# An mLSTM cell in front of a leaky-relu FFN on one core: transfers moved to ScalarE's queue, broadcasts joined into one request, and the last group's first product in float32r

## The chip, the cores and the metric

The kernel runs on one core of one Trainium2 chip. Times are device microseconds of one execution. The core's engines are TensorE (PE; its weight loads are listed apart as PEld), VectorE (DVE), ScalarE (ACT), GpSimd (POOL) and SyncE (SP). Each takes its instructions in order. Transfers are asked for by an engine's queue (SP's and ScalarE's here; a request is an instruction on that engine) and are carried out by sixteen DMA engines that the queues share.

## The reference

```
for t in range(768):                       # per batch b (4) and head h (8), head size D = 40
    m_new  = maximum(f[t] + m, i[t])
    f_stab = exp(f[t] + m - m_new);  i_stab = exp(i[t] - m_new)
    C = f_stab * C + i_stab * outer(v[t], k[t])
    n = f_stab * n + i_stab * k[t]
    y[t] = sigmoid(o[t]) * (C @ q[t]) / maximum(abs(n . q[t]), 1)
x = y as 3072 tokens x 320 features
h = x @ w_in                               # 320 x 2048
g = maximum(0.01 * h, h)
return g @ w_out                           # 2048 x 320
```

All inputs and the output are f32.

## The kernel before, in words

**Chunks, steps, groups.** The 768 tokens of a batch are cut into `NB` = 6 chunks `c` of 128. A step `s = 4*c + b` is one chunk of one of the four batches. The cell is computed chunk by chunk in matrix form with a state carried between chunks; the FFN of chunk `g` (its four steps together, 512 tokens, a "group") runs while the cells of chunk `g + 1` are computed. A loop (lines 1043 to 1103) gives out the work: 30 units of FFN for each group, 16 for the first product and 14 for the second, and after chosen units (`pairs`, line 1041) a piece of the next chunk's cells. The last group has no cells beside it.

**Order.** TensorE, DVE, ScalarE and POOL run in the order in which the program issues (`manual_schedule`, line 1022). SP's requests are ordered by the scheduler. A DMA signals on one of eight semaphore lanes, given out in turn, so that a request also waits until the DMA eight before it has landed.

**FFN.** The first product (`ff_units`, line 753) has eight pairs `j`: two PSUM banks `ph`, five slots of 64 rows on each of two row groups, 512 tokens moving (line 759), and a relu of each bank on ScalarE into `acts` (line 767). The second product (`fast_units`, line 824) is a fast scheme of seven products instead of eight, each for two token blocks `n`: p1, p1, p2, p2, p6, p6, p7, p7, p4, p4, p5, p5, p3, p3, eight matmuls each (line 835). Each product fills a bank `po`, which is emptied by ScalarE (p1, p6, p7, p4: copies at 854, 867, 875, 881) or DVE (p2, p5, p3: additions at 862, 887, 892). `ph` and `po` share the four banks of the pool `psf` in turn. The cells use four other banks, pool `psc`.

**Cells.** `load` (344) brings k with one request (356) and the values with four (359). `spread` (406) and `spread_q` (415) broadcast a row of gate factors of each batch from the scratch `a_dr` in HBM to 64 partitions, twice, into `w` and `ea` (lines 413 and 421). `u_mix` (684) multiplies state and gate-weighted queries (695), normalizes on DVE and POOL (702 to 713) and stores the step's x in the scratch `x_dr` with four requests of 20 rows (716). `gather_x` (719) reads it back with four requests (730) into `xT`, where the FFN of the next group reads it; it runs after the last unit of the first product (index 15) and later. All these requests are on SP. The last two steps' mixes stand after unit 19.

**Which lines the text uses.** 759 and 767 (first product, relu), 835 (second), 854 to 892 (its sums), 695 to 730 (mix, store, gather), 356, 359, 413, 421 (loads and broadcasts), 450 (POOL's product with `w`), 822 to 870 (DVE's sums of `acts` and weights), 249 to 263 (the weights' splitting at the start: masks, scaled sums, differences on DVE), 641 (a product with 128-column weights and 41 moving columns).

Of the kernel before, what the change touches and what calls it, by code (L numbers as in the profile page):

```python
# [10 lines left out]
U32 = mybir.dt.uint32  # L11
U64 = mybir.dt.uint64
AF = mybir.ActivationFunctionType
ALU = mybir.AluOpType
# [4 lines left out]
def kernel(  # L19
# [58 lines left out]
    dr = ctx.enter_context(tc.tile_pool(name="dr", bufs=1, space=bass.MemoryType.DRAM))  # L78

# [39 lines left out]
    kn = consts.tile([P, NL, H, DP], F32, name="kn")  # L119
    qn = consts.tile([P, NL, H, DP], F32, name="qn")  # L120
    S_t = [consts.tile([P, 2, H, DP], F32, name=f"S{n}") for n in range(NL)]
    S_v = [t[:].rearrange("p u h (k d) -> p u h k d", d=QW) for t in S_t]
    rb_t = [consts.tile([P, 3, RW], F32, name=f"rb{n}") for n in range(NR)]
    xb = consts.tile([P, PR * TB, QW], F32, name="xb")
# [147 lines left out]
    def gates(c):  # L272


        m0 = m0s.get(c)
        n = P if c == 0 else BH
        fc, il = (f0[:], i0[:]) if c == 0 else (fi[c][:, 0, :], fi[c][:, 1, :])
        F = wk.tile([n, P], F32, name="F", bufs=1)
        nc.vector.tensor_tensor_scan(F[:], fc, zeros[:n].to_broadcast([n, P]), 0.0, op0=ALU.add, op1=ALU.add)
        if c > 0:  # L280
            il_t = wk.tile([BH, P], F32, name="il", bufs=1)
            nc.vector.tensor_scalar(il_t[:], il, scalar1=m0[:], scalar2=None, op0=ALU.subtract)
            il = il_t[:]
        m = wk.tile([n, P], F32, name="m", bufs=1)
        nc.vector.tensor_tensor_scan(m[:], fc, il, -1e30 if c == 0 else 0.0, op0=ALU.add, op1=ALU.max)
        a = wk.tile([n, P], F32, name="a", bufs=1)
        nc.vector.tensor_tensor(a[:], F[:], m[:], op=ALU.subtract)
        bu = wk.tile([BH, 3, P], F32, name="bu", bufs=1)
        nc.vector.tensor_tensor(bu[:, 0, :], il[:BH], F[:BH], op=ALU.subtract)
        if c + 1 < NB:  # L290
            m1 = wk.tile([BH, 1], F32, name="m0")
            if c == 0:
                nc.vector.tensor_copy(m1[:], m[:BH, P - 1 :])
            else:
                nc.vector.tensor_tensor(m1[:], m0[:], m[:, P - 1 :], op=ALU.add)
            m0s[c + 1] = m1
        if c > 0:
            na = wk.tile([BH, 1], F32, name="na")
            nc.vector.tensor_tensor(na[:], m[:, SL - 1 : SL], F[:, SL - 1 : SL], op=ALU.subtract)
        bus[c] = bu, a, (na if c > 0 else None)  # L300

    def gates_exp(c):
# [9 lines left out]
        if c > 0:  # L312
            nc.sync.dma_start(a_dr[c, 0].rearrange("u n t -> n u t"), a[:].rearrange("n (u t) -> n u t", u=2))
            if c > 1:
                nc.sync.dma_start(a_dr[c, 1].rearrange("u n t -> n u t"), bu[:, 2, :].rearrange("n (u t) -> n u t", u=2))
            if 1 < c < NB - 2:
                load_fi(c + 2)
# [25 lines left out]

    def load(s):
        c, b = divmod(s, B)
        rows = ts(c, P)
        d = st.setdefault(s, {})
        n = s % NL
        d.update(k=kn[:, n], q=qn[:, n])
        if c == 0:  # L350
            d["va"] = S_t[n][:, 1]
            parts = [(d["k"][:, :, :D], k), (d["q"][:, :, :D], q), (d["va"][:, :, :D], v)]
            for dst, src in parts:
                nc.sync.dma_start(dst, src[b, :, rows, :].rearrange("h p d -> p h d"))
            return
        nc.sync.dma_start(d["k"][:, :, :D], k[b, :, rows, :].rearrange("h p d -> p h d"))
        for u in range(2):
            for i in range(2):
                nc.sync.dma_start(  # L359
                    S_v[n][ts(u, SL), u, :, i, :DB],  # L360
                    v[b, :, c * P + u * SL : c * P + (u + 1) * SL, DB * i : DB * (i + 1)].rearrange("h p d -> p h d"),
                )
# [42 lines left out]

    def spread(s):
# [3 lines left out]
        w = wk.tile([P, H, P], F32, name="w", bufs=NL)  # L410
        d["w"] = w[:].rearrange("p h t -> p (h t)")[:, : H * SL].rearrange("p (h t) -> p h t", t=SL)
        for u in range(2):
            nc.sync.dma_start(d["w"][ts(u, SL)], a_dr[c, 0, u, b * H : (b + 1) * H, :].partition_broadcast(SL))

    def spread_q(s):
# [3 lines left out]
        d["ea"] = wk.tile([P, H, SL], F32, name="ea", bufs=EAB)  # L419
        for r in range(2):  # L420
            nc.sync.dma_start(
                d["ea"][ts(r, SL)], a_dr[c, 1, 1 - r, b * H : (b + 1) * H, :].partition_broadcast(SL),
            )

    def spread_first(a, s2):
# [12 lines left out]
        for n in range(2):  # L438
            w = st[s2 + n]["w"] = wk.tile([P, H, P], F32, name="w", bufs=NL)
# [20 lines left out]
    def prep_vu(s):  # L460
# [3 lines left out]
        if s < NS:  # L464
            d["vu"] = wk.tile([P, H, 2, V1], F32, name="vu")
# [34 lines left out]
    def prep_kq(s):  # L500

        d = st[s]
        d["kqT"] = wk.tile([P, 2, PR * P], F32, name="kqT")
# [20 lines left out]
    def u_split(s):  # L524

        d = st[s]
        d["kqT"] = wk.tile([P, 2, PR * P], F32, name="kqT")
# [14 lines left out]
    def u_transpose(s):  # L542
        d = st[s]
        d["kqT"] = wk.tile([P, 2, PR * P], F32, name="kqT")
# [92 lines left out]
    def u_values(s):  # L637
# [4 lines left out]
        d["den"] = wk.tile([P, H], F32, name="den")  # L642
        denominators(d["den"][:], pa[:, :, D])

    def gate(s):

        d = st[s]
        d["x"] = wk.tile([P, Dm], F32, name="x")
# [7 lines left out]
    def u_plain(s):  # L656
# [13 lines left out]
        den = wk.tile([P, H], F32, name="den")  # L670
        denominators(den[:], hN[:, :, 0, DB])
        if b < 2:
            d["x"] = wk.tile([P, Dm], F32, name="x")[:]
# [10 lines left out]
    def u_mix(s):  # L684
# [16 lines left out]
        hb = wk.tile([P, PR * TB, QW], F32, name="hb", bufs=1)  # L701
        nc.vector.transpose(hb[:].rearrange("p (j n) d -> p j n d", n=TB), in_blocks(pT[:]))  # L702
        den = wk.tile([P, PR * TB], F32, name="den")
# [8 lines left out]
        xq = wk.tile([P, PR * P], F32, name="x")  # L712
# [6 lines left out]
    def gather_x(s):  # L719

        c, b = divmod(s, B)
        if ("xT", c) not in st:
            st["xT", c] = wk.tile([P, KC, GT], F32, name="xT", bufs=1)
        xT = st["xT", c]
        src = x_dr[s].rearrange("(k p) t -> p k t", p=DP)
        for r in range(2):
            at = 0
            while at < KC:
                k0, n = run_of(r, at)
                nc.sync.dma_start(xT[DP * r : DP * (r + 1), at : at + n, ts(b, P)], src[:, k0 : k0 + 2 * n - 1 : 2, :])  # L730
                at += n

# [20 lines left out]
    def ff_units(g):  # L753
        xT = st["xT", g]
# [59 lines left out]
        return firsts + fast_units(g)  # L814
# [104 lines left out]
    def ahead(s):  # L919

        if s < NS:
            if s < 2 * B:
# [99 lines left out]
    with tc.manual_schedule(engines={E.PE, E.DVE, E.Activation, E.Pool}):  # L1022
# [20 lines left out]
        for c in range(1, NB + 1):  # L1043
            if c > 1:
                ffs = ff_units(c - 1)
            cells = cell_units(c) if c < NB else []
            n_ff, n_c = len(ffs), len(cells)
            done = fed = 0
            waiting, after = [], []
            for i in range(n_ff):  # L1050
                if c == 1:
                    run(now, 2 if i < 10 else 3 if i < 14 else 4)
                    for n in fetch.get(i, ()):
                        load_weights(QN + n)
                    if i == 0:
                        prep_mask(B)
                        ahead(B)
                        load_fi(3)
                for s, steps in lazy.items():
                    if s in late and late[s] > 0:  # L1060
                        late[s] -= 1
                    else:
                        run(steps, 3)
                for n in masks.get(i, ()) if 1 < c < NB else ():
                    if c * B + n < NS:
                        prep_mask(c * B + n)
                ffs[i]()
                if c + 1 < NB:
                    if i == (1 if c == 1 else 0):
                        gates(c + 1)  # L1070
                    if c == 2 and i == 0:
                        mixed_weights()
                    if i == (3 if c == 1 else 2):
                        gates_exp(c + 1)
                upto = min(n_c, sum(p <= i for p in (place if c == 1 else pairs)))
                while done < upto:
                    fn, s = cells[done]
                    fn(s)
                    done += 1
                    if fn is u_mix:  # L1080
                        waiting.append(s)
                    if fn is u_plain and s < 2 * B - 1 or fn is u_parts and s == 2 * B - 1:
                        ahead(s + 1)
                    elif fn is u_mix:
                        after.append(s + 2)
                    elif fn is u_plain:
                        prep_mask(s + 2)
                        ahead(s + 2)
                if i >= NF - 1:
                    for s in waiting:  # L1090
                        gather_x(s)
                    waiting.clear()
                if i < NF or i >= NF + 8:
                    for s in after:
                        ahead(s)
                    after.clear()
                while fed < done:
                    fn, s = cells[fed]
                    fed += 1
                    if fn in (u_mix, u_plain):  # L1100
                        load_late(s + NR, 2)
                        if s + NL < NS:
                            feed(s + NL)
# [31 lines left out]
```

## Time and profile before

| what | us | where it is from |
|---|---|---|
| median of 3 runs | 511.85 | times (510.85 to 513.27) |
| the profiled execution's span | 508.0 | the page |
| TensorE busy | 492.0 (97%) | the page |
| DVE, ScalarE, POOL busy | 308.1, 171.5, 137.7 | the page |
| groups 1 to 4 of the FFN, start | 139.3, 214.2, 289.0, 365.2 | the trace's timeline |
| last group: start, first product, second product | 439.8, 34.5, 30.6 | the chain |

The runs' median is 3.85 us above the span of the one profiled execution; the span counts from the first to the last instruction that the trace records. A row of a group of instructions gives line, engine, operation, tiles and shape, count, then busy time and mean length, then the engine's idle time just before with what released it. The chain is read from top to bottom in time: start, length, what ran.

### The profile page before, as it was taken

The page shows a single profiled execution, that of the slowest core. Times are in us where ns is not written, and L with a number is a line of the kernel's source. Part 1 is how long each engine was busy: PE and PEld are TensorE (multiplying, and loading weights), DVE is VectorE, ACT ScalarE, POOL GpSimd, SP SyncE. Part 2 cuts the span into 40 slices and gives each one's busy share as a digit, 9 for nine tenths or more (in the row PEclk, how much of TensorE's full clock was granted, in tenths as well). Part 3 has the DMA queues.
Part 4 walks back from the last instruction along what each step waited for, and adds up shares of the span by engine and source line. Part 5 has one row for each costly group of instructions (what it writes and reads, how often), then busy time and mean ns, then how long its engine had stood idle before and what let it go on. Part 6 is the DMA issues. An engine that isn't in the chain of part 4 may idle for free.

```text
span 508.0 us, 12526 instructions
## 1 busy us (share of the span) xinstructions
PE 492.0 (97%) x4981; PEld 366.6 (72%) x4981; DVE 308.1 (61%) x515; ACT 171.5 (34%) x478; POOL 137.7 (27%) x175
## 2 busy tenths in 40 slices
PE   8878999999999999999999999999899999999997
PEld 7766878767655489955589855599755599744797
DVE  4779898899954778635765826764825664101321
ACT  3664864652722510323411323311213411022210
POOL 4243443360402404413104614014612003000020
PEclk9877999999999999999999999999999999999999
DMA  9977687888765551565663566564466212200001
GB/s 116 146 204 154 149 219 185 168 152 175 155 145 87 131 124 46 133 130 144 147 132 92 115 137 170 137 141 97 109 135 177 68 53 62 69 1 1 1 1 52
DMA packets 165290, 59.21 MB, mean 117 GB/s; under 512 B 128816, under 2 KB 156016, under 8 KB 165232
## 3 DMA queue, kind: packets, MB, share of 16 engines
q1 hardware_dynamic: 164848, 58.28, 52.2%
q8 instruction: 39, 0.64, 0.5%
q14 instruction: 19, 0.16, 0.1%
q10 hardware_dynamic: 384, 0.13, 0.1%
HBM read 51.68 MB, written 6.70 MB: 115 GB/s over the span
## 4 chain that ended last, share of the span: by engine, by line
PE 79%; DVE 9%; DMA 3%; ACT 3%; POOL 2%; issue 2%; SPq 2%; ACTq 0%; POOLq 0%; DVEq 0%
PE ph L759 36%; PE po L835 26%; PE po L794 6%; PE pT L695 3%; PE sd L614 3%; SPq L359 1%; PE sd L619 1%; DMA S<-in_v_dram 1%; ACT kqT L540 1%; PE tkq L548 1%; DVE raw L261 1%; DMA rb<-in_q_dram 1%; DMA w<-a_dr 1%; PE pa L641 1%; DVE qn L511 1%
## 5 line engine op out<-in xcount | busy, mean ns | idle before, releaser
L759 PE MATMUL ph<-xT,w_in 64*128 64x512 f32 (+1 forms) x1120 | 216.2, 538 | 2.4 <-DVE y L887 1.4
L759 PEld LDWEIGHTS ph<-xT,w_in 64*128 64x128 f32 x1120 | 108.6, 189 | 95.1 <-issue 86.3
L767 ACT ACTIVATE acts<-ph 128x512 f32<-128x512 f32 (+1 forms) x112 | 53.9, 533 | 179.0 <-PE ph L759 178.9
L835 PEld LDWEIGHTS po<-w_out,acts 128*128 128x128 f32 x640 | 87.3, 190 | 3.8 <-issue 3.8
L835 PE MATMUL po<-w_out,acts 128*128 128x160 f32 x640 | 89.1, 300 | 0.0
L450 POOL TENSOR_TENSOR w<-w,i 128x512 f32<-128x512 f32 x20 | 26.9, 1345 | 117.3 <-DMA w<-a_dr 117.2
L624 DVE TENSOR_TENSOR qn<-w,sd 64x512 f32<-64x512 f32 x40 | 27.4, 684 | 40.2 <-PE sd L619 20.5
L458 ACT ACTIVATE w<-w,gT 128x64 f32<-128x64 f32 (+1 forms) x192 | 50.8, 348 | 2.7 <-POOL w L450 1.7
L592 POOL TENSOR_TENSOR S<-S,f 40x336 f32<-40x336 f32 x36 | 32.0, 889 | 67.3 <-PE pT L695 36.3
L835 PE MATMUL po<-raw,acts 128*128 128x160 f32 x320 | 45.5, 300 | 0.0
L835 PEld LDWEIGHTS po<-raw,acts 128*128 128x128 f32 x320 | 43.9, 190 | 0.3
L794 PE MATMUL po<-w_out,acts 128*128 128x320 f32 x128 | 36.5, 436 | 0.0
L702 DVE STREAM_TRANSPOSE hb<-pT 128x512 f32<-128x512 f32 x16 | 11.5, 717 | 31.0 <-PE pT L695 30.8
L794 PEld LDWEIGHTS po<-w_out,acts 128*128 128x128 f32 x128 | 23.6, 190 | 9.3 <-issue 0.3
L511 DVE TENSOR_TENSOR qn<-kqT,ea 64x512 f32<-64x512 f32 x32 | 28.4, 888 | 1.0
L709 POOL TENSOR_TENSOR xb<-xb,den 128x320 f32<-128x320 f32 x16 | 11.7, 729 | 56.8 <-DVE xb L706 56.6
L596 DVE TENSOR_TENSOR S<-S,sd 40x336 f32<-40x336 f32 x36 | 18.1, 503 | 12.1 <-POOL S L592 11.2
L614 PEld LDWEIGHTS sd<-kqT 40*64 40x64 f32 x640 | 19.9, 135 | 6.1 <-issue 6.1
L822 DVE TENSOR_TENSOR raw<-acts 128x1024 f32<-128x1024 f32 x10 | 11.8, 1222 | 18.3 <-ACT acts L767 18.2
L713 DVE STREAM_TRANSPOSE x<-xb 128x512 f32<-128x512 f32 x16 | 18.2, 1140 | 7.6 <-POOL xb L709 7.6
L835 PE MATMUL po<-raw 128*128 128x160 f32 x160 | 22.5, 299 | 0.0
L835 PEld LDWEIGHTS po<-raw 128*128 128x128 f32 x160 | 22.0, 190 | 0.0
(151 smaller groups left out, 551.8 us busy)
## 6 DMA issues: line engine op xcount, KB each, us to landing
w<-a_dr SPq DMA_DIRECT2D x40, 128.0 KB
rb<-in_k_dram SPq DMA_DIRECT2D x64, 80.0 KB
rb<-in_q_dram SPq DMA_DIRECT2D x64, 80.0 KB
rb<-in_o_gate_dram SPq DMA_DIRECT2D x64, 80.0 KB
ea<-a_dr SPq DMA_DIRECT2D x32, 128.0 KB
kn<-in_k_dram SPq DMA_DIRECT2D x24, 160.0 KB
raw<-in_moe_w_out_dram SPq DMA_DIRECT2D x6, 640.0 KB
S<-in_v_dram SPq DMA_DIRECT2D x80, 40.0 KB
```

Source lines behind the costliest of these rows:

```text
L450: nc.gpsimd.tensor_tensor(w, w, cm2.unsqueeze(1).to_broadcast([P, H, SL]), op=ALU.add)
L458: yield nc.scalar.activation(w[:, h, :], w[:, h, :], AF.Exp, bias=gT[c][:, 0, bh : bh + 1], scale=1.0)
L511: nc.vector.tensor_tensor(mixed(s)[rows, 1 - r], d["kqT"][rows, 1].rearrange("p (h t) -> p h t", t=SL), d["ea"][rows], op=ALU.mult,)
L592: nc.gpsimd.tensor_tensor(new, old, g, op=ALU.mult)
L596: nc.vector.tensor_tensor(new, new, st[s]["dC", u], op=ALU.add)
L614: nc.tensor.matmul(bank[1 - u][toks, h, :], lhsT=kqT[rows, 0, ts(h, SL)], rhs=kqT[rows, 1, ts(h, SL)], start=True, stop=True,)
L624: nc.vector.tensor_tensor(mixed(s)[toks, u], w[toks], bank[1 - u][toks], op=ALU.mult)
L713: nc.vector.transpose(in_blocks(xq[:]), xb[:].rearrange("p (j n) d -> p j n d", n=TB))
L759: nc.tensor.matmul(ph[r][:, cols], lhsT=w_row(r, slot, j), rhs=xT[DP * r : DP * (r + 1), slot, cols], start=(slot == 0), stop=(slot == KC ...
L767: nc.scalar.activation(acts[:, f, cols], ph[r][:, cols], AF.Prelu, alpha=0.01)
L794: nc.tensor.matmul(po[n][:], lhsT=acts[:, f, ts(n, P)], rhs=w_out[:, f, :], start=(f == 0), stop=(f == NF - 1),)
L835: nc.tensor.matmul(bank[:], lhsT=left[:, f, :], rhs=right[:, f, :], start=f == 0, stop=f == KH - 1)
```

## The change

1. **Requests on ScalarE.** For chunks 3 and later, k and the values are no longer requested by `load` on SP but held as a generator in `later` and requested on ScalarE's queue: one request after each unit of a first product, two after each unit of a second. `ahead` requests at once what is still held. `gather_x` requests on ScalarE; one mixed step is gathered per unit, from the last unit of the first product.
2. **One request per broadcast.** `spread_rows` writes 128 partitions from two rows with one request where there were two of 64 partitions. The two halves of the second gate factor are stored in swapped order, by two requests instead of one.
3. **The last group's first product.** After two pairs as before, each of the other six pairs is three float32r products: `raw` times `raw` and `low` times `low` in the banks `ph`, `dif` times `dif` in two banks `pe` of `psc`. The mask 0xFFFFF000 keeps the top bits of a number; `low` is what it cuts off (scaled by 4096 for w_in, with its sign turned), and `dif` is the number plus a multiple of that part. A ScalarE copy scaled by -EPS, a DVE scaled sum and a ScalarE relu combine them, each per bank.
4. **Preparing that.** When group 4's mixes are issued (after unit 19), the cells' pools are closed and their memory is given to the parts (`open_parts`). Four requests on SP copy w_in to `raw` (128 x 1280 f32 each). Eight halves of w_in are split, each by a DVE mask, a POOL subtraction, a DVE scaled sum and a ScalarE scaled copy; x is split by three DVE passes for each of four steps. These steps are given out two per unit of group 4's second product and three per unit of group 5's first, behind the products' own work.
5. The unit loop is rewritten (placements as before: 30 per group), and the cells' tiles move to pools of their own, `cc` and `cw`.

```diff
+    def bring_later(n):
+        while n > 0 and later:
+            s = next(iter(later))
+            next(later[s][0], None)
...
+        if c < 3:
+            for _ in bring(nc.sync):
+                pass
+        else:
+            later[s] = [bring(nc.scalar), 5]
...
+    def spread_rows(to, rows):
+
+        nc.sync.dma_start(
+            to.rearrange("p h t -> p (h t)"),
+            rows.unsqueeze(1).to_broadcast([2, SL, H, SL]).rearrange("u p h t -> u p (h t)"),
+        )
...
-        for u in range(2):
-            nc.sync.dma_start(d["w"][ts(u, SL)], a_dr[c, 0, u, b * H : (b + 1) * H, :].partition_broadcast(SL))
+        spread_rows(d["w"], a_dr[c, 0, :, b * H : (b + 1) * H, :])
...
-        for r in range(2):
-            nc.sync.dma_start(
-                d["ea"][ts(r, SL)], a_dr[c, 1, 1 - r, b * H : (b + 1) * H, :].partition_broadcast(SL),
-            )
+        spread_rows(d["ea"][:], a_dr[c, 1, :, b * H : (b + 1) * H, :])
...
-                nc.sync.dma_start(xT[DP * r : DP * (r + 1), at : at + n, ts(b, P)], src[:, k0 : k0 + 2 * n - 1 : 2, :])
+                nc.scalar.dma_start(xT[DP * r : DP * (r + 1), at : at + n, ts(b, P)], src[:, k0 : k0 + 2 * n - 1 : 2, :])
...
+    def top_bits(dst, src):
+        nc.vector.tensor_scalar(
+            dst.bitcast(U32), src.bitcast(U32), scalar1=0xFFFFF000, scalar2=None, op0=ALU.bitwise_and,
+        )
...
+        def first():
+            t = tmp_part()[:].rearrange("p k t -> p (k t)")
+            held.append(t)
+            top_bits(t, src)
+            nc.gpsimd.tensor_tensor(t, t, src, op=ALU.subtract)
+
+        def second():
+            t = held[0]
+            nc.vector.scalar_tensor_tensor(
+                parts["w", "dif"][n][:, at], in0=t, scalar=1.0 + 1.0 / EPS, in1=src, op0=ALU.mult, op1=ALU.add,
+            )
+            nc.scalar.activation(parts["w", "low"][n][:, at], t, AF.Copy, scale=1.0 / EPS)
...
+        top_bits(t, src)
+        nc.vector.tensor_tensor(low, t, src, op=ALU.subtract)
+        nc.vector.scalar_tensor_tensor(
+            parts["x", "dif"][:, :, cols], in0=low.bitcast(F32), scalar=1.0 + 1.0 / EPS, in1=src, op0=ALU.mult, op1=ALU.add,
+        )
...
+            def first():
+                ph.extend(psf.tile([P, GT], F32, name=f"ph{r}", tag="mm") for r in range(2))
+                rows(j, ph, "raw", True, False)
+
+            def second():
+                rows(j, ph, "low", False, True)
+
+            def third():
+                pe.extend(psc.tile([P, GT], F32, name=f"pe{r}", tag="c") for r in range(2))
+                rows(j, pe, "dif", True, True)
+                fs = [acts[:, f_of(r, j), :] for r in range(2)]
+                for r in range(2):
+                    nc.scalar.activation(fs[r], pe[r][:], AF.Copy, scale=-EPS)
+                for r in range(2):
+                    nc.vector.scalar_tensor_tensor(
+                        fs[r], in0=ph[r][:], scalar=1.0 + EPS, in1=fs[r], op0=ALU.mult, op1=ALU.add,
+                    )
+                for r in range(2):
+                    nc.scalar.activation(fs[r], fs[r], AF.Prelu, alpha=0.01)
...
+                gather()
+                if t <= ENDS < upto:
+                    open_parts()
+                    for n in range(QN):
+                        fetch_w_part(n)
+                    todo = split_steps()
+                t = max(t, upto)
+                bring_later(1 if i < len(firsts) else 2)
+                prepare(3 if i < len(firsts) else 2)
```

## The prediction

> **What bounds the kernel now.** First the page's shares, the slices and the chain.
>
> ```profile
> PE 492.0 (97%) x4981; PEld 366.6 (72%) x4981; DVE 308.1 (61%) x515; ACT 171.5 (34%) x478; POOL 137.7 (27%) x175
> PE   8878999999999999999999999999899999999997
> DVE  4779898899954778635765826764825664101321
> PEclk9877999999999999999999999999999999999999
> DMA  9977687888765551565663566564466212200001
> PE 79%; DVE 9%; DMA 3%; ACT 3%; POOL 2%; issue 2%; SPq 2%; ACTq 0%; POOLq 0%; DVEq 0%
> ```
>
> TensorE is the bound: 97% busy, at full clock after the fourth slice. Any gain has to shorten its work; anything that makes it wait is a loss. DVE is light only in the last six slices, the DMA engines only in the last nine. The windows, one per FFN group (busy by engine, clock, DMA share):
>
> ```profile
> 139.30:214.20 74.90, 74.90 (x777) 54.24 (x776) 49.35 (x76) 21.45 (x65) 21.27 (x25) 1.00 0.49 109
> 289.00:365.20 76.20, 74.86 (x775) 54.15 (x774) 46.42 (x78) 21.14 (x64) 23.56 (x26) 1.00 0.58 130
> 365.20:439.80 74.60, 74.54 (x706) 54.11 (x706) 36.74 (x64) 16.26 (x44) 12.17 (x16) 1.00 0.41 100
> ```
>
> TensorE fills each group; the waits that a faster queue could remove are at most 1.3 us in one group. The rest of the view of waits agrees: the largest of TensorE's waits is 1.8 us, and almost all lie in the start-up. SP's waits (second fence) cost nothing: SP does only transfers.
>
> ```profile
> PE ph L759 <- DVE y L887: 1.4, 1, 1.4
> SPq L716 <- DVE x L713: 29.8, 11, 8.6
> SPq L730 <- PE ph L759: 8.6, 1, 8.6
> ```
>
> The first line matters: a group's first product waits for the DVE addition that empties a bank of `psf`. These four banks are handed round in order, so a second product (2.19 us: 30.64/14 below) needs the bank of the product four before it. The end of the chain, and ScalarE in the second half of the fourth group:
>
> ```profile
> 417.86 21.93 PE po L835 x160
> 439.79 34.53 PE ph L759 x160
> 474.33 30.64 PE po L835 x224
> ```
> ```profile
> 420.27 0.30 ACT L867 COPY y<-po 128x160 f32<-128x160 f32 x1 [7.71 <-PE po L835]
> 422.44 0.29 ACT L867 COPY y<-po 128x160 f32<-128x160 f32 x1 [1.88 <-PE po L835]
> 424.62 0.29 ACT L875 COPY hn<-po 128x160 f32<-128x160 f32 x1 [1.88 <-PE po L835]
> ```
>
> Each copy begins the moment its product ends, because ScalarE has nothing else there. SP issues the transfers of x:
>
> ```profile
> 420.85 5.10 SPq L716 DMA_DIRECT2D x_dr<-x  x8
> 426.11 6.08 SPq L730 DMA_DIRECT2D xT<-x_dr  x8
> ```
>
> **Part 1: float32r products, gain.** The last group's first product is 34.53 us for eight pairs, 4.32 each: five slots of two row groups, 0.86 us a slot. Six pairs become three products of five slots. No float32r product is in the trace. The edit splits each operand into a top and a low half; an f32 product is four half-products, so one of them costs 0.86/4 = 0.215 us a slot, 3.22 us for three products, and 6 x (4.31 - 3.22) = 6.5 us are saved. The bound above is two of the four: 6.4 us a pair, +12.9 us. If weight loading does not overlap (line 641's 128-column weights come every 0.107 us), 4.83 us a pair: +3.1. I take -6.4: in the trace the two row groups' loads start 6 ns apart and lie wholly under the products. The added combination is, per pair, four ScalarE passes of 0.55 us (the relus of line 767) and two DVE passes of 0.6 to 0.7: under 3.22, hidden.
> The Trainium skill, "FP8 and Floating Point Precision", section "TensorE Precision Notes", gives true f32 four passes; by it the price is also -6.4, and no run here shows it yet.
>
> **Part 2: gathers and loads on ScalarE, loss.** SP loses 64 gathers (median 0.607 us), 12 loads of k (0.50) and 48 of values (0.63); TensorE hardly waited for SP, so I price that at 0; what stays on SP (spreads, stores of x, outputs) only moves ahead, and its stores wait for DVE anyway (29.8 us above). ScalarE takes them in order, and behind them stand copies that empty banks. Call the end of the last mix product T0 (417.86 in group 4, 192.24 in group 1). After it ScalarE's order is: four gathers of the third step, a load of k, a load of values, the first p6 copy, four gathers of the fourth step, two loads, the second p6 copy, then two loads before each p7 copy. The third step's stores land at T0+5.7 by the trace's semaphore events, the fourth's at T0+9.3 (+10.3 in group 1, whose stores are issued 1 us later). The fourth gather and the load of k also wait for the DMA eight back on their semaphore lane, which are the fourth step's first two stores (T0+8.4 to +10). So: the first p6 copy ends at T0+10.6 to +12.2, and p4, which needs its bank, would start at T0+8.76 (four products): 1.9 to 3.4 us. The next four gathers (2.4), two values (1.25) and the copy (0.3) end at T0+14.6 to +16.2, against p4's second half at T0+12.8 to +14.3: another 2 us. Groups 1 to 3: 3.9 to 5.4 each, 4.8 with the p7 copies' rest; 14.4 in all. Group 4 has no loads left: the gathers of its third step end about T0+8.3, so its first p6 copy is in time; those of the fourth (landed 427.2, 2.4 of issue) and one low-half pass put the second copy at 430.75: 2.0. Bounds: 1 us in all if issuing holds ScalarE for nothing and only the landings count; 24 if every issue takes twice its median, as some in the trace do (maximum 1.46). In the firsts a single transfer (0.6) stands between relus 4.3 us apart: 0.
>
> **Part 3: splitting in group 4.** After the mix the memory of the cell pools is reused, so DVE's first masking waits for the fourth step's stores (427.2). Then DVE does, in order: six masks of 128x640 (0.49, line 259), two relu sums (1.25), four scaled sums (0.87, near line 261's 0.89), and four splits of x (0.49+0.90+0.87): 2.9+2.5+3.5+9.1 = 18.0 us, to 445.2. Only then come p5's additions, which empty the two banks for group 5's first pair: second one about 448.5. TensorE would start that pair at 439.8+2.0 = 441.8: it waits 6.7 us. Bounds: 1.5 (DVE at its fastest rows) to 10.5 (20% slower beside POOL, as line 870's passes here, 1.38 against 1.22). In before DVE had 36.74 us of work in 74.6: this cover is gone in the last 20 us. POOL's eight subtractions, about 1.5 each (line 450's 1.27 is for 512 elements, these have 640), lie beside DVE. The four 655 KB copies of w_in have 22 us and idle DMA engines: 0.
>
> **Part 4: one request per spread.** 72 DMAs become 36, and four become eight: SP's time, 0. A spread moves the same 128 rows of 2,048 bytes. What this does to the engines is rival 2.
>
> **Sum.** 508.0 - 6.4 + 14.4 + 2.0 + 6.7 = 524.7 us of span; the median of the runs (511.85) lies 3.85 above the profiled span, so 528.6; I say 528.5, 3.3% slower.
>
> **Rivals.**
> 1. *The copies are not late* (the other side, faster). Place: the first p6 copy. If the fourth step's stores land 2 us earlier because SP is free, and issues overlap ScalarE's copies, the three groups cost 0.3 us each (a copy's own length, with the stores landed at T0+8.8), group 4 nothing, group 5 its lower bound of 1.5: 508.0 - 6.4 + 1 + 1.5 = 504.1, with 3.85 outside the span 508.0, 0.8% faster (505.5 to 509.3). It decides when both copies of p6 end before T0+9 and T0+11. Against it: ScalarE's order is fixed, and L730's issues last 0.6 us in SP.
> 2. *Spreads on few DMA engines.* Each store of x has 20 rows, and its semaphore shows 11 increments (ten engines and one for the rest), all others, of 64 or 128 rows, 16: the engines follow the slowest dimension. The new spread's source has slowest dimension 2. On two engines its 128 packets (84 ns each) take 5.4 us instead of 0.7. Eight a group are 43 us on those two; the other traffic takes 0.5 of each engine, 35 us: 78 of 75 us. Queues would fill, gathers and w come late: 3 us a group by the overflow alone, 9 in all, and a burst of two spreads ahead of a gather delays it by 10.8; 5 to 20 us more, 534 to 548, say 538. For it: the increments. Against: w had slack (its longest hold of TensorE's path is 3.33 us), and the share is a mean.
> The Trainium skill, "DMA: Bandwidth & Descriptors", section "Why a DMA increments its semaphore by 16 and not by 1", states just this rule: as many engines, up to 16, as divide both slowest dimensions. The eleven increments agree; by it this rival's 43 us stand.
> 3. *float32r at half speed or without overlap*: +9.5 to +19 on the sum, 538 to 548. Against it: hidden loads.
> 4. *Losses and gain cancel*: Part 2 at 4 us with group 4, Part 3 at 2: 508.0 - 6.4 + 6 + 3.85 = 511.5, within 0.5% (509.3 to 514.4).
>
> **Chances.** Forecast 0.47; rival 1 0.16; rival 2 0.22; rival 3 0.08; rival 4 0.07. Rival 3 and 2 are slower, as is the forecast: 0.77; beyond 0.5%, which is what a measurement of this kernel can tell, faster holds 0.16, unchanged 0.07. The range leaves out the faster half of rival 1 and the tail of rivals 2 and 3: 507 to 544. The forecast's own range (518 to 534) comes from Part 2 at 6 to 20 and Part 3's bounds.
>
> **What would show it.** Right: ScalarE's p6 copies 2 to 4 us behind their products, TensorE waits in its second products for ScalarE in groups 1 to 3, one wait of some 7 us at the start of the last group released by DVE, six triples of 3.2 us there. Rival 2: spreads landing 5 us after issue and POOL's products with w waiting longer. Wrong: no second-product waits, or triples over 4.3 us; then Part 2 or Part 1 fails. A gain in groups 1 to 4 would refute the claim that SP held nothing up.

## The result and the profile after

The changed kernel takes 596.5 us against 511.4 for the kernel before: 1.168 times as long, 95% interval 1.162 to 1.173. The profiled execution's span is 594.7 us against 508.0. The prediction had the sign right and the size wrong: 528.5 us, with a range that ended at 544.

Lines of the page of the changed kernel: slices, queues and the chain's shares by engine.

```profile
PEclk9669997997899798799997799997799999869999
DMA  8765745646632642842643752543660213310001
q1 hardware_dynamic: 115320, 51.72, 35.4%
q10 hardware_dynamic: 49472, 9.31, 8.8%
PE 43%; DMA 26%; SPq 10%; DVE 9%; ACTq 3%; issue 2%; ACT 2%; POOL 2%; DVEq 0%; POOLq 0%
```

TensorE held 79% of the chain before; it now holds 43%, and DMA landings with SP's queue hold 36%, against 5% before. The DMA engines as a whole are less busy (the two large queues, q1 and q10, take 44.2% together, against 52.3%), so this is not a lack of bandwidth over all sixteen. The clock, steady before after the fourth slice, now drops again and again.

The windows of the changed kernel, one per FFN group (busy by engine, clock, DMA share, GB/s):

```profile
158.70:256.20 97.50, 82.57 (x777) 62.66 (x776) 48.14 (x82) 21.37 (x65) 22.22 (x27) 0.89 0.50 109
256.20:347.60 91.40, 80.55 (x777) 58.84 (x776) 45.84 (x81) 20.82 (x64) 20.72 (x27) 0.93 0.50 111
347.60:439.20 91.60, 81.00 (x777) 59.54 (x776) 45.74 (x80) 20.82 (x64) 20.82 (x27) 0.93 0.49 111
439.20:528.50 89.30, 78.17 (x707) 55.60 (x706) 57.15 (x84) 20.13 (x50) 25.18 (x21) 0.96 0.26 78
528.50:594.70 66.20, 62.97 (x442) 52.81 (x442) 24.78 (x34) 20.10 (x38) 5.83 (x8) 0.96 0.05 18
```

Groups 1 to 4 take 97.5, 91.4, 91.6 and 89.3 us where they took 74.9, 74.8, 76.2 and 74.6. Of these 69 us, 46 are time in which TensorE stands still; the other 23 are longer busy time for the same number of products, at the lower clock of the last column but two. The start-up is 19.4 us longer (158.7 against 139.3). Only the last group is shorter. TensorE's largest waits after the start-up, from the view of waits (line 979 is the second product, 1011 p6's copy, 730 the mix, 903 the first product, 1031 p5's additions):

```profile
PE po L979 <- ACT y L1011: 20.7, 5, 6.2
PE pT L730 <- DVE f L345: 14.3, 3, 5.2
PE ph L903 <- DVE y L1031: 7.8, 2, 7.0
```

The first and the third were forecast in their places, at 1.9 to 3.4 us each and 6.7 us; the first reaches 6.2 us. What stands behind most of the rest is in the chain of waits of the changed kernel:

```profile
179.25 13.09 DMA w<-a_dr
209.41 8.74 DMA ea<-a_dr
229.30 7.14 DMA x_dr<-x
271.69 10.74 DMA kn<-in_k_dram
300.93 8.47 DMA ea<-a_dr
```

On this chain the spreads take 8 to 13 us to land, and stores of x and loads of k, whose requests did not change in size, take 7 to 11.

### The profile page after: what moved, and what is told of

Read it like the earlier page. It is cut to its first block, busy times and chain, and to the rows that moved or that the text cites. A ratio compares the mean times of both kernels' runs of the same rounds, so it can differ in the third digit from the quotient of the medians.

```text
span 594.7 us, 12699 instructions
## 1 busy us (share of the span) xinstructions
PE 517.6 (87%) x5041; PEld 396.8 (67%) x5041; DVE 336.4 (57%) x555; ACT 184.0 (31%) x498; POOL 148.3 (25%) x183
## 4 chain that ended last, share of the span: by engine, by line
PE 43%; DMA 26%; SPq 10%; DVE 9%; ACTq 3%; issue 2%; ACT 2%; POOL 2%; DVEq 0%; POOLq 0%
PE ph L903 18%; PE po L979 14%; DMA S<-in_v_dram 4%; DMA rb<-in_k_dram 4%; DMA x_dr<-x 4%; PE po L938 3%; SPq L233 3%; DMA ea<-a_dr 3%; PE ph L840 2%; DMA rb<-in_o_gate_dram 2%; DMA w<-a_dr 2%; ACTq L765 2%; DMA xT<-x_dr 2%; DMA kn<-in_k_dram 2%; DMA raw<-in_moe_w_out_dram 2%
## 5 line engine op out<-in xcount | busy, mean ns | idle before, releaser
L903 PE MATMUL ph<-xT,w_in 64*128 64x512 f32 (+1 forms) x1000 | 201.5, 550 | 12.6 <-DVE y L1031 7.8
L903 PEld LDWEIGHTS ph<-xT,w_in 64*128 64x128 f32 x1000 | 104.7, 197 | 94.8 <-issue 70.2
L911 ACT ACTIVATE acts<-ph 128x512 f32<-128x512 f32 (+1 forms) x100 | 47.5, 525 | 147.1 <-PE ph L903 124.5
L979 PE MATMUL po<-raw,acts 128*128 128x160 f32 x320 | 58.4, 350 | 20.7 <-ACT y L1011 20.7
L979 PEld LDWEIGHTS po<-raw,acts 128*128 128x128 f32 x320 | 55.3, 230 | 22.7 <-ACT y L1011 22.2
L1031 DVE TENSOR_TENSOR hn<-hn,po 128x160 f32<-128x160 f32 x10 | 3.2, 320 | 60.9 <-POOL hn L1026 46.7
L730 PE MATMUL pT<-qn,S 128*64 128x64 f32 x512 | 19.8, 241 | 14.3 <-DVE f L345 14.3
L730 PEld LDWEIGHTS pT<-qn,S 128*64 128x64 f32 x512 | 18.2, 154 | 17.9 <-issue 17.8
L1011 ACT COPY y<-po 128x160 f32<-128x160 f32 x10 | 2.9, 290 | 82.9 <-DMA xT<-x_dr 74.8
L1012 POOL TENSOR_TENSOR y<-y,raw 128x160 f32<-128x160 f32 x10 | 6.4, 639 | 88.0 <-ACT y L1011 88.0
L737 DVE STREAM_TRANSPOSE hb<-pT 128x512 f32<-128x512 f32 x16 | 11.4, 713 | 28.7 <-PE pT L730 28.5
L546 DVE TENSOR_TENSOR qn<-kqT,ea 64x512 f32<-64x512 f32 x32 | 26.2, 818 | 0.8
L540 DVE STREAM_TRANSPOSE kqT<-rb 128x512 f32<-128x512 f32 x32 | 20.8, 686 | 6.0 <-DMA rb<-in_q_dram 5.7
```

The costliest lines, as they stand in the source:

```text
L540: nc.vector.transpose(d["kqT"][:, i].rearrange("p (h t n) -> p h n t", n=TS, t=QW), raw_blocks(s, i, QW).rearrange("p (h n) d -> p h n d", ...
L546: nc.vector.tensor_tensor(mixed(s)[rows, 1 - r], d["kqT"][rows, 1].rearrange("p (h t) -> p h t", t=SL), d["ea"][rows], op=ALU.mult,)
L730: nc.tensor.matmul(pT[DP * r : DP * (r + 1), j * P + u * SL : j * P + (u + 1) * SL], lhsT=S[:, u, h, :], rhs=m[:, u, h, :], start=True, st ...
L903: nc.tensor.matmul(ph[r][:, cols], lhsT=w_row(r, slot, j), rhs=xT[DP * r : DP * (r + 1), slot, cols], start=(slot == 0), stop=(slot == KC ...
L911: nc.scalar.activation(acts[:, f, cols], ph[r][:, cols], AF.Prelu, alpha=0.01)
L979: nc.tensor.matmul(bank[:], lhsT=left[:, f, :], rhs=right[:, f, :], start=f == 0, stop=f == KH - 1)
```

## The experiments

Three parts had to be told apart: the one-request spread, the requests on ScalarE, and the float32r products with their preparation. Theory A says that the spread on two DMA engines makes most of the loss. Theory B gives it to ScalarE's queue.

**Undoing the spread, and making only it.** The first kernel is the changed one with

```
 def spread_rows(to, rows):
-    nc.sync.dma_start(to..., rows.unsqueeze(1).to_broadcast([2, SL, H, SL])...)
+    for u in range(2):
+        nc.sync.dma_start(to[ts(u, SL)], rows[u].partition_broadcast(SL))
```

> The changed kernel with each broadcast as two requests of 64 partitions again (source and destination then have slowest dimension 64); all else as changed. Theory A (the one-request broadcast runs on two DMA engines, and these two, nearly full, make every landing late): the loss of the chain of DMA landings goes, about 65 of the 85 us; 525 to 532 us remain (ScalarE's blocking 12 to 16, group 5's start 7, float32r -5), and w lands within 3 us. Theory B (ScalarE's queue is what costs: gathers and loads in front of copies): the kernel stays above 570.

Measured: 537.9 us, 1.055 of the kernel before (1.049 to 1.060). 58 of the 85 us go with this edit (0.113 of 509). Counted as below, w lands 2.5 us after its request in the median and 3.0 at most (12 requests), as expected. What remains is above the forecast of 525 to 532.

The second is the kernel before with `spread_rows` as in the change and the swapped store, nothing else.

> The kernel before with the one-request broadcast alone (and the second factor's halves stored swapped by two requests). Theory A: most of the loss by itself, 565 to 585 us, start-up later by about 19 us and each of groups 1 to 3 longer by 12 to 18. Theory B: unchanged within 0.5%, 509 to 514.

Measured: 585.4 us, 1.149 (1.145 to 1.154): +76 us by this part alone, and 58 where it is undone: the parts do not simply add up. Theory B is out. Start-up is 23 us longer, groups 2 and 3 take 101.0 and 99.5 us, while groups 1 and 4 keep theirs within about 1 us (76.0 and 74.4). Groups 2 and 3 hold eight spreads each, group 1 six and group 4 four. The chain of waits of this kernel, inside group 2 (239 to 340 us; SPq L360 is a values request, L399 one for k, q or o in blocks):

```profile
243.85 7.75 DMA w<-a_dr
251.68 0.64 SPq L360
...
253.67 7.86 DMA rb<-in_k_dram
261.59 8.41 DMA ea<-a_dr
270.02 0.31 SPq L399
270.43 8.12 DMA ea<-a_dr
...
294.82 7.91 DMA ea<-a_dr
...
304.15 7.74 DMA w<-a_dr
```

The landings stand in a row. A spread takes eight us; a request behind it on SP waits for its semaphore lane, so SP stands still; the request after that is again a spread or, as its late landing suggests, lies behind one in the engines' queues. SP's waits for DMA landings add up to 57 us here and 5 us in the kernel before (sum of its view of waits). By the semaphore events, the median from the end of a request to its landing, after the start-up, goes from 2.5 to 7.5 us for w and from 2.6 to 7.5 for ea, and with them from 1.9 to 6.3 for the o gates and from 2.2 and 2.6 to 7.5 and 7.4 for the two halves of the outputs, which did not change at all (counted on the lanes whose number of events comes out exactly). ScalarE then waits for o gates in front of p6's copies, and TensorE for these copies (views of waits of this kernel; 871 is p6's copy):

```profile
ACT rb L498 <- DMA rb<-in_o_gate_dram: 67.0, 7, 18.3
PE po L839 <- ACT y L871: 23.5, 2, 12.1
```

**Is it two engines, or one large request?** The third kernel keeps two requests of 64 partitions and writes each source as 2 x 32 repeats:

```
-nc.sync.dma_start(to[ts(u, SL)], rows[u].partition_broadcast(SL))
+nc.sync.dma_start(to[ts(u, SL)]..., rows[u]...to_broadcast([2, SL // 2, H, SL])...)
```

> The first kernel (e1: two requests of 64 partitions, 537.9 us) with each request's source written as 2 x 32 repeats instead of 64: the same requests, rows and bytes, only the source's slowest dimension is 2. Theory A (the number of DMA engines is what divides both slowest dimensions): two engines again, three semaphore increments per request, and the time goes back to that of the changed kernel, 580 to 600 us. Theory C (one large request in place of two, or the swapped store of the second factor, is what costs): as e1, 534 to 541.

Measured: 602.0 us, 1.181 (1.175 to 1.186). The same rows, bytes and number of requests as in the first kernel, and the same packets (7,168 of 2,048 bytes in both traces): 64 us more. It is the slowest dimension. The count of semaphore events says how many engines: with 3 increments per spread (two engines, one for the rest), 11 per store of x and 16 for all others, all eight lanes' totals of this kernel come out exactly (1,052 on one, 1,091 on the next, and so on). In the changed kernel six lanes come out exactly and two within two of 1,100. The Trainium skill, "DMA: Bandwidth & Descriptors", section "Why a DMA increments its semaphore by 16 and not by 1", gives the rule: as many engines, up to 16, as divide the slowest dimension of both sides. The runs agree, and show that a stride-0 dimension counts like any other.

**Requests on ScalarE.** The next kernel is the first without float32r (`THREE = ()`, no `open_parts`).

> As the first of these kernels (two requests per broadcast), without float32r and its preparation; gathers and loads stay on ScalarE. Both theories take the part of ScalarE's queue from it. By the terms of the prediction: 511 + 14.4 + 2 = 527, 521 to 533; if ScalarE's blocking costs under 1 us a group, 512 to 514.

Measured: 526.3 us, 1.037 (1.029 to 1.044): +17 us against the forecast 16.4. ScalarE's timeline of this kernel after the mix in group 1, whose last product ends at 189.4 us (the number in brackets is ScalarE's idle time before, and who ended it):

```profile
195.10 3.67 ACTq L763 DMA_DIRECT2D xT<-x_dr  x4
199.27 0.43 ACTq L380 DMA_DIRECT2D kn<-in_k_dram  x1
199.80 0.61 ACTq L384 DMA_DIRECT2D S<-in_v_dram  x1
200.45 0.29 ACT L1009 COPY y<-po 128x160 f32<-128x160 f32 x1 [12.85 <-DMA xT<-x_dr]
200.53 2.58 ACTq L763 DMA_DIRECT2D xT<-x_dr  x4
203.33 1.29 ACTq L384 DMA_DIRECT2D S<-in_v_dram  x2
204.67 0.29 ACT L1009 COPY y<-po 128x160 f32<-128x160 f32 x1 [3.93 <-DMA xT<-x_dr]
```

And TensorE's there:

```profile
200.79 2.44 PE L977 MATMUL po<-raw,acts 128*128 128x160 f32 x16 [2.53 <-ACT y L1009]
205.01 2.44 PE L977 MATMUL po<-raw,acts 128*128 128x160 f32 x16 [1.78 <-ACT y L1009]
```

The two p6 copies end 11.4 and 15.6 us after the mix (forecast 10.6 to 12.2 and 14.6 to 16.2), and the two waits are 2.5 and 1.8 us (forecast 1.9 to 3.4 and 2). In all, TensorE waits 13.0 us for p6's copies in groups 1 to 3 and 2.6 in group 4.

Gathers and loads apart: the first kernel with `later[s] = [bring(nc.sync), 5]` (loads back on SP), with `nc.sync` in `gather_x` (gathers back), and with both.

> As e1 with k and the values on SP again; the gathers stay on ScalarE. e1 is at 537.9 and with both on SP it is 528.9, so the two parts hold 9 us together. By the prediction's order the copy waits for stores to land only because of the gathers: most of the 9 stays here, 534 to 537, and TensorE's waits for the p6 copy (18.1 us in e1) stay above 9. Rival: the loads are the larger part, 529 to 532.

> As e1 with the gathers on SP again; k and the values stay on ScalarE. Most of the 9 us goes, 529 to 532, and TensorE's waits for the p6 copy fall to about 3 us (the one in group 4 that the kernel with both on SP has). Rival: loads that wait for their semaphore lane hold the copies as well, 534 to 538.

> As the first of these kernels, with the gathers and the loads of k and values on SP as well: what is left is the float32r products, their preparation and the rewritten loop. Theory A: 511 - 5 (float32r) + 7 (group 5 waits for DVE) = 513, 510 to 517. Theory B: the same, since here nothing is on ScalarE; it differs from the first kernel by 12 to 16 us under A, by over 50 under B.

Measured: 531.8 (1.042, 1.036 to 1.048), 519.8 (1.019, 1.014 to 1.024) and 528.9 us (1.037, 1.031 to 1.043). All three expectations failed in their times. With the gathers back on SP and the loads on ScalarE, 18 us of the first kernel's go, not 6 to 9: the gathers are the main cost. With the loads back and the gathers left, 6 us go, and TensorE's waits for p6's copy fall from 18.1 to 12.5 us: beside gathers on ScalarE the loads cost too. With both on SP the kernel is not at 513 but 9 us slower than with the loads on ScalarE. What the loads cost thus depends on where the gathers stand. In the rewritten loop the loads that a step asks for are issued ahead of the gathers; on SP they then delay the gathers, and the next group's first product waits for x: 3.2 us in the trace with both on SP, whose execution, the fastest of its four, is 5 us slower than the profiled one with the loads on ScalarE. A later kernel (the first with four float32r pairs, below) shows the extreme of it, since it asks for the loads at once, on SP. SP's timeline there, and TensorE's wait:

```profile
206.43 2.68 SPq L384 DMA_DIRECT2D S<-in_v_dram  x4
209.16 1.26 SPq L441 DMA_DIRECT2D w<-a_dr  x2
210.47 5.16 SPq L763 DMA_DIRECT2D xT<-x_dr  x8
```
```profile
PE ph L901 <- DMA xT<-x_dr: 19.1, 3, 7.9
```

In the kernel before the same gathers start at 201.5 us, ahead of all the loads. Loads on ScalarE alone, with no float32r:

> Two requests per broadcast, gathers on SP, k and values on ScalarE, no float32r and no preparation: of the change only the loads' move and the rewritten loop are left. If the loads cost nothing and the gathers made the whole of Part 2's loss: 509 to 513, TensorE's waits in groups 1 to 4 under 3 us together. With the gathers on ScalarE as well the same kernel took 526.3. Rival: loads in front of the copies cost as the prediction had it, 515 to 522.

Measured: 508.8 us, 0.997 (0.994 to 1.000). With the gathers on SP, the move of the loads and the rewritten loop cost nothing.

**float32r and its preparation.** So the kernel with the gathers on SP and the loads on ScalarE (519.8) differs from this one (508.8) by float32r alone: +11 us. Its view of waits, and windows around the start of the last group (the clock is the last column but two):

```profile
PE ph L901 <- DVE y L1029: 8.4, 2, 7.6
PE po L977 <- ACT y L1009: 2.9, 1, 2.9
```
```profile
446.10:456.40 10.30, 5.24 (x10) 2.03 (x12) 10.02 (x15) 1.47 (x2) 5.03 (x5) 0.50 0.09 32
456.40:515.00 58.60, 58.57 (x436) 50.61 (x432) 21.35 (x30) 19.37 (x37) 3.96 (x7) 1.00 0.04 15
```

The wait for DVE is there (7.6 and 0.8 us), DVE is busy without a break, and a stretch of 10.2 us at half clock lies across it, 6.1 us of it after TensorE has begun again. The wait for p6's copy (line 1009) comes from the preparation, since no gather is on ScalarE here: the first scaled copy of the splitting stands ahead of p6's copy and begins only at 429.54 us, when DVE's mask and POOL's subtraction are done; the copy follows at 430.18. Can the preparation be hidden? The next kernel (loads and gathers on SP) begins all splitting after p5's additions, splits only the parts of w_in that are read, and keeps four float32r pairs (it also asks for each step's loads at once and gathers all mixed steps at once):

```
-        LEAD = 2
+        LEAD = 4
-            halves = [(n, half) for n in range(QN) for half in range(2)]
+            halves = [(n, half) for n in range(LEAD // 2, QN) for half in range(2)]
...
-                prepare(3 if i < len(firsts) else 2)
+                prepare(3 if i < len(firsts) else 2 if i >= 27 else 0)
```

> Two requests per broadcast; gathers and loads on SP as in the kernel before; float32r for the last four pairs only, parts of w_in split only where they are read, and all splitting begun after p5's additions are given to DVE. If the loss that remains with all on SP (528.9 against 509.3) is DVE and ScalarE being late before group 5, with the half clock that follows each long wait, it goes: 4 x 0.83 (triples of 3.48 us in the changed kernel's trace) = 3.3 us faster than before, 505 to 508. If the float32r products or the rewritten loop cost by themselves, it stays at 513 or above.

Measured: 535.4 us, 1.051. This run told nothing on float32r, because its loads asked for at once on SP delayed the gathers, as shown above; group 5 itself started without a wait for DVE (462.0 us, right behind the second products). The same was therefore made on the kernel with the loads on ScalarE, with two steps per unit and a split's second half at least two steps behind its first, for four, five and six float32r pairs (`LEAD` 4, 3, 2).

> The kernel with gathers on SP and loads on ScalarE (519.8), float32r for the last four pairs, splitting only what is read and begun after p5's additions, two steps per unit. If the loss there is only DVE and ScalarE being late before group 5 with the half clock behind it: no wait over 1.5 us at group 5's start, full clock to the end, 4 x 0.83 = 3.3 us below the kernel without float32r: 506 to 509. Rival (float32r products cost by themselves): 511 or above.

> The same with five float32r pairs: 5 x 0.83 = 4.2 us of gain if the splitting is still in time (13 us from p5's additions to the end of the third f32 pair and the second products left): 505 to 508. If DVE is late for the fourth pair: a wait of some us there, 508 to 514.

> The same with all six float32r pairs of the change: 5.0 us of gain at most, 504 to 507; more probably the third pair waits for the split of x (four times 2.6 us on DVE, three of them after p5), 2 to 5 us with a half clock after it: 508 to 514.

Measured: 506.4 us, 0.992 (0.989 to 0.995); 507.4, 0.997 (0.994 to 1.000); 506.1, 0.995 (0.992 to 0.999). The intervals of the three overlap; the first and third are faster than the kernel before by their intervals, by under 1%. Against the kernel without float32r (508.8) the medians are 2.4, 1.4 and 2.7 us lower, less than 0.85 us a pair; of the three intervals, each overlaps that kernel's. The six-pair kernel did not meet the 508 to 514 that were held more probable: no wait for the split of x is in its trace, and its third triple waits 1.4 us for DVE's combination (the five-pair kernel's, 1.5). The end of the chain of the four-pair kernel:

```profile
419.85 21.93 PE po L977 x160
441.78 17.38 PE ph L901 x78
459.59 2.09 PE ph L838 x17
463.07 1.86 PE ph L838 x16
...
469.97 1.85 PE ph L838 x16
473.43 30.64 PE po L977 x224
```

Group 5 begins the moment group 4 ends (441.78), the clock stays at 1.00, and triples come every 3.46 us. So in this trace float32r saves 0.85 us a pair (4.31 less 3.46). What cost 11 us was the order, pace and amount of its preparation: the six-pair kernel differs from the one at 519.8 in these alone.

## Why the prediction was wrong

Undone one after another, the parts account for the loss: the spread 58 us (1.168 to 1.055), the gathers on ScalarE 18 (to 1.019), float32r with its preparation 11 (to 0.997), the loads nothing. The shares depend on this order: undone first, the loads hold 6 us.

**The step that failed is Part 4, which stands in the sum at 0,** with the price of rival 2, where its cost was put. The joined spread cost 58 us undone and 76 alone. The rival's mechanism was right: two engines, by slowest dimension; a spread lands in 7.5 us or more, of which 5.4 were forecast as the time of its packets. Its price, "3 us a group by the overflow alone ... 5 to 20 us", was worked out as throughput: 78 us of work for two engines in 75 us. What counted is latency: in the chain above the landings follow one another, and 78 us of work would leave the two engines idle for over a fifth of the 101 us that group 2 took. SP's queue is in order, each request waits for the one eight before, and so the 5 extra us of each spread are paid one after another: by this estimate eight spreads a group can add 40, and other landings behind them come late too. Groups 2 and 3 of the kernel with this edit alone lost 26.2 and 23.3 us, some eight times the 3 us of overflow; 12.1 of these 49.5 us are products at a lower clock (TensorE is busy for 80.5 and 81.3 us where it was for 74.8 and 74.9). And the rival had no term for the start-up, which lost 23 us. "Against: w had slack" held for a single landing, not for a row of them. The chance of 0.22 was the second mistake: eleven increments on a store of 20 rows were evidence in hand, and nothing in the trace spoke against the rule. Only whether it would cost was open.

**Part 1** was right in mechanism, and a little large: 6.4 us forecast, 6 x 0.85 = 5.1 measured, since a triple takes 3.46 and not 3.22 us (the whole kernel shows 2.7 for six pairs). Half speed or no overlap (rival 3) is out: 3.46 us is under their bounds. (Line 641's weights come every 0.112 us in the trace, not 0.107, which moves that bound alone.)

**Part 2** was right: 16.4 us forecast, 17 measured without float32r (18 with it), with the two waits at the places and of the sizes named (14.4 and 2.0 forecast, 13.0 and 2.6 in the trace, which has one half-clock stretch of 3.4 us beside them). But how it splits was not seen: without the gathers the loads go to ScalarE free, and they free SP for the gathers (9 us in the rewritten loop), against "SP's waits cost nothing", priced at 0.

**Part 3** was right in the wait (6.7 forecast; 7.6 + 0.8, and 7.0 + 0.8 in the changed kernel) and wrong in what goes with it. Part 1 and Part 3 made +0.3; float32r cost 11. Of the 10.7 us between, group 4's second products are 4.2 (37.1 us against 32.9), the half clock 3.0 (half of 6.1 us), the wait 1.7 and the smaller gain 1.3. About 0.5 us is not accounted for. The prediction had 2.0 us in group 4, but in Part 2 and mostly for the gathers; the splitting by itself, ahead of p6's copy, had no term. No step of the prediction priced the clock after a wait.

**The forecast without the spread**, 528.5, compares with 1.055 x 511.4 = 539 measured; those 10 us are about what float32r and its preparation cost beyond their terms. Rival 1 failed in its condition: the copies were late as reckoned. Its time (505.5 to 509.3) is reached at 506.4, but by other means: the gathers on SP and the preparation later.

## What to carry to other kernels

Joining requests into one saves queue time only if the joined access pattern still spreads over the DMA engines: look at the slowest dimension of both sides, stride-0 repeats included, before counting requests, and price a slow transfer by the landings that stand behind it in an in-order queue, not by bytes. A request that waits must not stand on an engine ahead of work that empties a bank; loads did no harm there once no waiting request stood in the same queue. Preparation for a later stage belongs after the last instruction that the bound engine waits for, and a wait of TensorE of over 3 us that it causes should be priced with a stretch at half clock behind it.

## What the runs showed that was not expected

A wait of TensorE can cost more than its length. In the changed kernel, around group 5's start (windows; the clock is the last column but two):

```profile
510.30:523.90 13.60, 8.35 (x62) 8.10 (x60) 13.23 (x16) 2.77 (x6) 9.39 (x7) 1.00 0.05 20
523.90:534.20 10.30, 7.72 (x16) 3.04 (x18) 10.06 (x14) 2.21 (x3) 4.61 (x3) 0.50 0.13 49
534.20:560.90 26.70, 26.70 (x207) 19.89 (x203) 8.70 (x12) 14.15 (x25) 0.00 (x0) 1.00 0.02 7
```

Up to TensorE's last product, the half-clock stretches of all these runs last 3.4 us or a multiple of it. A short wait can be enough for one: with all requests on SP, TensorE waited about 2.0 us for x at the start of group 4, in a window in which it worked 1.34 of 3.30 us, and the next 3.4 us ran at half clock:

```profile
363.70:367.00 3.30, 1.34 (x5) 0.57 (x6) 0.32 (x1) 0.00 (x0) 0.00 (x0) 1.00 0.54 126
367.00:370.40 3.40, 3.40 (x10) 1.61 (x10) 0.00 (x0) 0.00 (x0) 0.00 (x0) 0.50 0.74 94
```

In the kernel before, a wait of 1.4 us at the same place left the clock alone. The Trainium skill, "TensorE: Matmul & The Clock Gate", section "Part 1: The HAM clock gate (the "warmup" mystery)", has the clock halve after an idle window of some 3.4 us; the length of the stretches agrees, but here a window that was two fifths busy was followed by one too.

The traces give the condition more closely. In each of the fourteen, the half-clock stretches begin and end on one grid of 3.413 us. Laid over the traces from 60 us on, it has 40 windows at full clock in which TensorE was busy for 40% of the time or less: the clock was half in the next window after every one of them. Of the 1,740 windows busy for 59% or more it was after none, and of the 29 between after 7. So it matters how a wait lies on the grid. All 37 waits of TensorE over 3 us came with such a stretch, at the latest 3.4 us behind them, 9 of the 23 between 1.4 and 3 us, and none of the six between 1.0 and 1.3; the waits of 7 us before group 5 came with 10.2 us each. (Busy is as the profile models it.)

A float32r product of a pair of row groups with 512 columns took 3.46/15 = 0.231 us and not a quarter of the f32 one's 0.86. Why was not tried.
